# Linear attention feeding a gated MLP on one core: attention on head pairs with nine tokens per partition, the next batch placed by hand between the MLP's groups

## The chip, the cores and the metric

The kernel runs on one core of one Trainium2 chip. The metric is the device time of one execution in microseconds, given as the median of several runs. Profiles come from one profiled execution. Engines are called as the profile calls them: PE (TensorE matmuls), PEld (its weight loads), DVE (VectorE), ACT (ScalarE), POOL (GpSimd) and SP (SyncE, which here only issues DMAs).

## What is computed

Eight batches of eight heads, 576 tokens and 64 features go through an attention without softmax, in which relu of q and of k is weighted by the cosine and the sine of the token's position; the result, with its heads side by side, is the input x (4608 x 512) of a two-layer MLP ("MoE" in the names) with a swish between.

```python
theta = np.pi / 2.0 * np.arange(S) / S                      # S = 576
def phi(x, c, s):
    r = np.maximum(x, 0.0)
    return np.concatenate([r * c, r * s], axis=-1)          # 64 -> 128 features
q_p, k_p = phi(q, cos_w, sin_w), phi(k, cos_w, sin_w)
kv = np.einsum('bhsf,bhsd->bhfd', k_p, v)
z = np.sum(k_p, axis=2)
num = np.einsum('bhsf,bhfd->bhsd', q_p, kv)
den = np.einsum('bhsf,bhf->bhs', q_p, z)[..., None] + 1e-06
x = (num / den).transpose(0, 2, 1, 3).reshape(B * S, H * D)  # 4608 x 512
h = x @ w_in                                                # w_in 512 x 2048
out = (h * (1.0 / (1.0 + np.exp(-beta * h)))) @ w_out       # w_out 2048 x 512
```

Inputs and the output are float32; the matmuls of both kernels run in bfloat16. Both compute `Silu(beta * h)` and divide row j of `w_out` by `beta[j]` when it is cast.

## The kernel before

**Attention** (`attention_batch`, L111). One batch is taken in five pieces of up to 128 tokens (the last has 64), with a token on each partition and the eight heads side by side. Per piece, k, v and q are loaded in runs of 64 floats (L127; k on SP's queue, v on ACT's, q on both in turn). ACT writes `k_p` with two relu activations, one scaled by cosine, one by sine (L137, L139); DVE does the same for `q_p` (L143, L146) and casts v (L151), and POOL sets a 65th column to one, which yields z. For each head PE adds `k_p`ᵀ `v` to `kv_ps` (L156, 65 columns) and transposes `q_p` (L166), and DVE copies the transposes out (L174). Behind the five pieces `kv_ps` is copied to SBUF (L179); then each piece and head has a matmul `num_ps` (L189, 65 columns), a reciprocal of its 65th column (L198), the division (L204), four transposes of `x_sb` (L220) and ACT's copy into `xt_all` (L228), the whole transposed x.

**MoE** (`moe_chunk`, L233). A chunk is 512 tokens, and there are nine. For each of 16 slices of 128 hidden features, four matmuls of 512 columns fill `h_ps` (L239, two PSUM buffers) and ACT's Silu makes `g_t` (L247). Then each of the chunk's four groups of 128 tokens has 16 matmuls into `o_ps` (L257, one PSUM buffer, but in the last two chunks two that belonged to `num_ps`), a copy by DVE (L265) and an output DMA on POOL's queue (L266).

**Weights.** `load_w_in` (L94) and `load_w_out` (L103) load float32 pieces into two staging buffers and DVE casts them (L100, L108); `w_out` comes on POOL's queue in 16 pieces.

**Order.** The calls at the end (L268 to L281) are: w_in, batch 0, w_out, batch 1, and then each batch followed by those chunks whose tokens are ready. That order is only a priority: the framework's scheduler arranges the instructions of each engine and moves matmuls of later work up into gaps.

Of the kernel before, what the change touches and what calls it, by code (L numbers as in the profile page):

```python
# [13 lines left out]
ALU = mybir.AluOpType  # L14

USE_XBAR_X = False
# [3 lines left out]
def kernel(  # L20
# [9 lines left out]
):  # L30
    nc = tc.nc

    B, H, S, D = q.shape
    P = 128
    NT = B * S
# [4 lines left out]
    HG = H // 2  # L40
    NCH = (S + P - 1) // P
    SC = [min(P, S - n * P) for n in range(NCH)]
    TCH = 512
    NTC = NT // TCH
    TT = TCH // P

    const_pool = ctx.enter_context(tc.tile_pool(name="const", bufs=1))
    xt_pool = ctx.enter_context(tc.tile_pool(name="xt", bufs=1))
    win_pool = ctx.enter_context(tc.tile_pool(name="win", bufs=1))
    wout_pool = ctx.enter_context(tc.tile_pool(name="wout", bufs=1))  # L50
    kvz_pool = ctx.enter_context(tc.tile_pool(name="kvz", bufs=2))

    raw_pool = ctx.enter_context(tc.tile_pool(name="raw", bufs=4))
    kp_pool = ctx.enter_context(tc.tile_pool(name="kp", bufs=3))
    qpt_pool = ctx.enter_context(tc.tile_pool(name="qpt", bufs=2))
    xsb_pool = ctx.enter_context(tc.tile_pool(name="xsb", bufs=3))
    rden_pool = ctx.enter_context(tc.tile_pool(name="rden", bufs=4))
    gt_pool = ctx.enter_context(tc.tile_pool(name="gt", bufs=18))
    osb_pool = ctx.enter_context(tc.tile_pool(name="osb", bufs=3))

    kv_psum_pool = ctx.enter_context(tc.tile_pool(name="kvps", bufs=1, space=bass.MemoryType.PSUM))
    tps_psum_pool = ctx.enter_context(tc.tile_pool(name="tps", bufs=1, space=bass.MemoryType.PSUM))
    num_psum_pool = ctx.enter_context(tc.tile_pool(name="numps", bufs=1, space=bass.MemoryType.PSUM))
    moeh_psum_pool = ctx.enter_context(tc.tile_pool(name="moehps", bufs=2, space=bass.MemoryType.PSUM))
    moeo_psum_pool = ctx.enter_context(tc.tile_pool(name="moeops", bufs=1, space=bass.MemoryType.PSUM))

    ident = const_pool.tile([P, P], BF16)
    make_identity(nc, ident)

    iota_t = const_pool.tile([P, NCH], FP32)  # L70
    nc.gpsimd.iota(iota_t, pattern=[[P, NCH]], base=0, channel_multiplier=1,
                   allow_small_or_imprecise_dtypes=True)

    ANG = math.pi / (2.0 * S)
    sin_cols = const_pool.tile([P, NCH], FP32)
    cos_cols = const_pool.tile([P, NCH], FP32)
    halfpi = const_pool.tile([P, 1], FP32)
    nc.vector.memset(halfpi, math.pi / 2.0)
    zero_b = const_pool.tile([P, 1], FP32)
    nc.vector.memset(zero_b, 0.0)  # L80
    nc.scalar.activation(sin_cols, iota_t, AF.Sin, bias=zero_b, scale=ANG)
    nc.scalar.activation(cos_cols, iota_t, AF.Sin, bias=halfpi, scale=-ANG)

    beta_sb = const_pool.tile([P, JT], FP32)
    nc.sync.dma_start(out=beta_sb, in_=moe_beta.rearrange("(j p) -> p j", p=P))
    rbeta_sb = const_pool.tile([P, JT], FP32)
    nc.vector.reciprocal(rbeta_sb, beta_sb)

    xt_all = xt_pool.tile([P, MI, NT], BF16, name="xt_all")

    win_bf = []
    wout_bf = []

    def load_w_in(staging):  # L94
        for mi in range(MI):
            w_stage = staging.tile([P, DF], FP32, name="w_stage", tag="w_stage")
            eng = nc.sync if mi % 2 == 0 else nc.scalar
            eng.dma_start(out=w_stage, in_=moe_w_in[mi * P : (mi + 1) * P, :])
            wt = win_pool.tile([P, DF], BF16, name=f"win{mi}")
            nc.vector.tensor_copy(wt, w_stage)  # L100
            win_bf.append(wt)

    def load_w_out(staging):  # L103
        for jc in range(JT):
            wo_stage = staging.tile([P, DM], FP32, name="wo_stage", tag="wo_stage")
            nc.gpsimd.dma_start(out=wo_stage, in_=moe_w_out[jc * P : (jc + 1) * P, :])
            wo = wout_pool.tile([P, DM], BF16, name=f"wout{jc}")
            nc.vector.tensor_scalar_mul(wo, wo_stage, rbeta_sb[:, jc : jc + 1])  # L108
            wout_bf.append(wo)

    def attention_batch(b):  # L111
        kv_ps = [
            kv_psum_pool.tile([P, HG, D + 1], FP32, name=f"kv_ps{g}", tag=f"kv_ps{g}")
            for g in range(2)
        ]
        qpt_sb = qpt_pool.tile([P, H, S], BF16, name="qpt_sb")

        for n in range(NCH):
            sc = SC[n]
            raws = {}  # L120
            for name, src, eng in (
                ("k", k, nc.sync),
                ("v", v, nc.scalar),
                ("q", q, nc.sync if n % 2 == 0 else nc.scalar),
            ):
                t = raw_pool.tile([P, H, D], FP32, name=f"raw_{name}", tag=f"raw_{name}")
                eng.dma_start(  # L127
                    out=t[:sc],
                    in_=src[b, :, n * P : n * P + sc, :].rearrange("h p d -> p h d"),
                )  # L130
                raws[name] = t
            raw_k = raws["k"][:sc]
            raw_q = raws["q"][:sc]
            raw_v = raws["v"][:sc]

            k_p = kp_pool.tile([P, H, 2, D], BF16, name="k_p", tag="k_p")
            nc.scalar.activation(k_p[:sc, :, 0, :], raw_k, AF.Relu,  # L137
                                 scale=cos_cols[:sc, n : n + 1])
            nc.scalar.activation(k_p[:sc, :, 1, :], raw_k, AF.Relu,  # L139
                                 scale=sin_cols[:sc, n : n + 1])  # L140

            q_p = kp_pool.tile([P, H, 2, D], BF16, name="q_p", tag="q_p")
            nc.vector.tensor_scalar(q_p[:sc, :, 0, :], raw_q,  # L143
                                    scalar1=cos_cols[:sc, n : n + 1], scalar2=0.0,
                                    op0=ALU.mult, op1=ALU.max)
            nc.vector.tensor_scalar(q_p[:sc, :, 1, :], raw_q,  # L146
                                    scalar1=sin_cols[:sc, n : n + 1], scalar2=0.0,
                                    op0=ALU.mult, op1=ALU.max)

            v_sb = kp_pool.tile([P, H, D + 1], BF16, name="v_sb", tag="v_sb")  # L150
            nc.vector.tensor_copy(v_sb[:sc, :, 0:D], raw_v)  # L151
            nc.gpsimd.memset(v_sb[:sc, :, D : D + 1], 1.0)

            for h in range(H):
                g, hg = divmod(h, HG)
                nc.tensor.matmul(  # L156
                    kv_ps[g][:, hg, :],
                    lhsT=k_p[:sc, h, :, :],
                    rhs=v_sb[:sc, h, :],
# [152 lines left out]
```

## Time and profile before

| | us |
|---|---|
| median of 3 runs | 384.47 |
| lowest, highest run | 381.54, 386.7 |
| profiled execution, span from first to last instruction | 381.9 |
| PE busy in it (2272 matmuls) | 322.9 |
| DVE busy (395 instructions) | 150.5 |
| ACT busy (268 instructions) | 169.3 |
| POOL busy (99 instructions) | 36.6 |

The span is the profiled execution's own time; it lies among the times of the runs, and no time around it is given apart from it. PE's busy row counts a matmul until its modelled end, so that matmuls overlap in it and a full row still can hide short waits. For those the starts of successive matmuls are compared. 46.53 MB go through the DMA queues, 115472 of 119340 packets being smaller than 512 bytes.

### The profile page before, as it was taken

How to read it: one execution, taken by the hardware profiler on the slowest of the kernel's cores; microseconds unless marked ns; L12 is line 12 of the kernel's file. 1: busy time of each engine (PE TensorE's matmuls, PEld its weight loads, DVE VectorE, ACT ScalarE, POOL GpSimd, SP SyncE). 2: the span in 40 equal slices, each digit the busy share in tenths (PEclk: the TensorE clock that was granted, in tenths of full speed). 3: DMA queues.
4: the chain of work that ended last, by engine and by line, in shares of the span. 5: the costliest groups of instructions: out<-in, count | busy, mean ns of one | idle time of the engine just before them, and what ended most of it. 6: DMA issues, size and time to landing. Idle time of an engine off the chain costs nothing.

```text
span 381.9 us, 5842 instructions
## 1 busy us (share of the span) xinstructions
PE 322.9 (85%) x2272; PEld 165.8 (43%) x2272; DVE 150.5 (39%) x395; ACT 169.3 (44%) x268; POOL 36.6 (10%) x99
## 2 busy tenths in 40 slices
PE   0130265799989999999999999999999999999993
PEld 0020243555445555455545545554555444444441
DVE  0551484753664268255405743750346011020020
ACT  1133046077447734770753595257306613604600
POOL 2021131000110020001001100110010011011011
PEclk9999999599999999999999999999999999999999
DMA  8999969533996399469208956410010011011011
GB/s 259 313 278 223 235 178 225 80 70 87 234 245 127 70 223 231 96 155 232 60 0 192 197 101 135 124 57 0 29 55 30 0 56 56 0 57 55 1 57 55
DMA packets 119340, 46.53 MB, mean 122 GB/s; under 512 B 115472, under 2 KB 115472, under 8 KB 118800
## 3 DMA queue, kind: packets, MB, share of 16 engines
q1 hardware_dynamic: 60720, 16.79, 23.0%
q10 hardware_dynamic: 54432, 15.73, 20.2%
q0 software_dynamic: 4160, 13.63, 11.0%
q8 instruction: 18, 0.29, 0.3%
q14 instruction: 10, 0.08, 0.1%
HBM read 36.71 MB, written 9.44 MB: 121 GB/s over the span
## 4 chain that ended last, share of the span: by engine, by line
PE 48%; issue 28%; DMA 14%; DVE 5%; POOL 2%; ACT 1%; POOLq 0%; ACTq 0%; DVEq 0%
PE h_ps L239 22%; PE o_ps L257 17%; DMA wo_stage<-in_moe_w_out_dram 10%; DMA raw_q<-in_q_dram 4%; PE num_ps L189 3%; PE t_ps L166 3%; PE t_ps L220 2%; POOL out_dram L266 2%; PE kv_ps L156 2%; DVE o_sb L265 1%; DVE q_p L143 1%; DVE q_p L146 1%; DVE qpt_sb L174 1%; DVE wout L108 1%; DVE x_sb L204 0%
## 5 line engine op out<-in xcount | busy, mean ns | idle before, releaser
L239 PE MATMUL h_ps<-xt_all,win 128*128 128x512 bf16 x576 | 148.2, 384 | 0.4 <-ACT g_t L247 0.3
L247 ACT ACTIVATE g_t<-h_ps,beta_sb 128x512 bf16<-128x512 f32 x144 | 98.5, 688 | 97.6 <-PE h_ps L239 93.4
L257 PE MATMUL o_ps<-wout,g_t 128*128 128x512 bf16 x448 | 105.8, 379 | 0.3
L257 PEld LDWEIGHTS <-g_t 128*128 128x128 bf16 x576 | 56.0, 98 | 65.8 <-issue 0.9
L239 PEld LDWEIGHTS <-win 128*128 128x128 bf16 x576 | 52.2, 98 | 56.4 <-issue 9.5
L265 DVE COPY o_sb<-o_ps 128x512 f32<-128x512 f32 x28 | 19.3, 689 | 81.3 <-PE o_ps L257 81.3
L166 PE MATMUL t_ps<-ident,q_p 128*128 128x128 bf16 (+1 forms) x320 | 27.6, 231 | 27.9 <-DVE q_p L143 17.5
L137 ACT ACTIVATE k_p<-raw_k,cos_cols 128x512 bf16<-128x512 f32 (+1 forms) x40 | 28.7, 717 | 46.4 <-PE kv_ps L156 22.2
L228 ACT COPY xt_all<-t_ps 128x512 bf16<-128x512 bf16 (+1 forms) x40 | 21.7, 542 | 44.0 <-PE t_ps L220 34.9
L174 DVE COPY qpt_sb<-t_ps 128x1024 bf16<-128x1024 bf16 (+1 forms) x40 | 25.2, 630 | 35.8 <-PE t_ps L166 35.6
L166 PEld LDWEIGHTS <-q_p 128*128 128x128 bf16 (+1 forms) x320 | 21.2, 106 | 35.6 <-DVE q_p L143 17.5
L156 PE MATMUL kv_ps<-v_sb,k_p 128*128 128x65 bf16 (+1 forms) x320 | 20.0, 206 | 19.4 <-DVE v_sb L151 17.9
L266 POOL DMA_DIRECT2D out_dram<-o_sb x36 | 19.7, 547 | 156.0 <-DVE o_sb L265 123.3
L204 DVE TENSOR_TENSOR x_sb<-num_ps,rden 128x256 bf16<-128x256 f32 (+1 forms) x80 | 31.2, 414 | 1.0
L139 ACT ACTIVATE k_p<-raw_k,sin_cols 128x512 bf16<-128x512 f32 (+1 forms) x40 | 28.4, 711 | 0.0
L257 PE MATMUL o_ps_tail<-wout,g_t 128*128 128x512 bf16 x128 | 28.0, 379 | 0.0
L156 PEld LDWEIGHTS <-k_p 128*128 128x128 bf16 (+1 forms) x320 | 16.3, 105 | 26.7 <-issue 17.6
L189 PE MATMUL num_ps<-kvz_sb,qpt_sb 128*128 128x65 bf16 (+1 forms) x320 | 24.0, 203 | 1.2 <-DVE x_sb L204 0.8
L265 DVE COPY o_sb<-o_ps_tail 128x512 f32<-128x512 f32 x8 | 5.5, 691 | 49.2 <-PE o_ps_tail L257 49.2
L189 PEld LDWEIGHTS <-qpt_sb 128*128 128x128 bf16 (+1 forms) x320 | 17.9, 106 | 8.6 <-DVE x_sb L204 3.1
L220 PE MATMUL t_ps<-ident,x_sb 128*128 128x128 bf16 (+1 forms) x160 | 19.0, 223 | 3.1 <-DVE x_sb L204 3.0
L143 DVE TENSOR_SCALAR q_p<-raw_q,cos_cols 128x512 bf16<-128x512 f32 (+1 forms) x40 | 18.9, 475 | 6.6 <-DMA raw_q<-in_q_dram 6.6
(23 smaller groups left out, 99.5 us busy)
## 6 DMA issues: line engine op xcount, KB each, us to landing
out_dram<-o_sb POOLq DMA_DIRECT2D x36, 256.0 KB, 3.0
raw_v<-in_v_dram ACTq DMA_DIRECT2D x32, 256.0 KB, 4.7
raw_k<-in_k_dram SPq DMA_DIRECT2D x32, 256.0 KB, 6.8
wo_stage<-in_moe_w_out_dram POOLq DMA_DIRECT2D x16, 256.0 KB, 5.9
raw_q<-in_q_dram ACTq DMA_DIRECT2D x16, 256.0 KB, 5.0
raw_q<-in_q_dram SPq DMA_DIRECT2D x16, 256.0 KB, 6.8
w_stage<-in_moe_w_in_dram SPq DMA_DIRECT2D x2, 1024.0 KB, 8.3
w_stage<-in_moe_w_in_dram ACTq DMA_DIRECT2D x2, 1024.0 KB, 8.1
```

What stands on the lines that cost most here:

```text
L137: nc.scalar.activation(k_p[:sc, :, 0, :], raw_k, AF.Relu, scale=cos_cols[:sc, n : n + 1])
L139: nc.scalar.activation(k_p[:sc, :, 1, :], raw_k, AF.Relu, scale=sin_cols[:sc, n : n + 1])
L156: nc.tensor.matmul(kv_ps[g][:, hg, :], lhsT=k_p[:sc, h, :, :], rhs=v_sb[:sc, h, :], start=(n == 0 and hg == 0), stop=(n == NCH - 1 and hg ...
L166: nc.tensor.matmul(qpt_ps[:, h, 0:sc], lhsT=q_p[:sc, h, :, :], rhs=ident[:sc, :sc], is_transpose=True, start=(h == 0), stop=(h == H - 1),)
L174: nc.vector.tensor_copy(qpt_sb[:, :, n * P : n * P + sc], qpt_ps[:, :, 0:sc])
L189: nc.tensor.matmul(num_ps[g][:sc, hg, :], lhsT=qpt_sb[:, h, n * P : n * P + sc], rhs=kvz_sb[:, h, :], start=(hg == 0), stop=(hg == HG - 1),)
L204: nc.vector.tensor_tensor(x_sb[:sc, hs, :], num_ps[g][:sc, :, 0:D], rb, op=ALU.mult,)
L239: nc.tensor.matmul(h_ps, lhsT=win_bf[mi][:, jt * P : (jt + 1) * P], rhs=xt_all[:, mi, t0 : t0 + TCH], start=(mi == 0), stop=(mi == MI - 1),)
L247: nc.scalar.activation(g_t, h_ps, AF.Silu, scale=beta_sb[:, jt : jt + 1])
L257: nc.tensor.matmul(o_ps, lhsT=g_tiles[jt][:, tt * P : (tt + 1) * P], rhs=wout_bf[jt], start=(jt == 0), stop=(jt == JT - 1),)
L265: nc.vector.tensor_copy(o_sb, o_ps)
L266: nc.gpsimd.dma_start(out=out[t0 + tt * P : t0 + (tt + 1) * P, :], in_=o_sb)
```

## The change

Everything in the kernel function is rewritten; the computation stays.

- **Layout.** Heads are taken in pairs: head 2j on partitions 0 to 63, head 2j + 1 on 64 to 127. Each partition holds nine consecutive tokens of its head, so that one piece of a load is 9 x 64 floats, 2304 bytes. Tokens are worked on in the order n, p (token 9p + n), and the output's view undoes that: a group of 128 goes out in two DMAs of 64 rows. All loads are issued on SP's queue, the outputs on POOL's, and from chunk 6 on SP's.
- **Weights of position.** Cosine and sine are put on v rather than on k (`v_scale`, nine instructions each, with the cosine or sine itself as 65th column), so k and q need one relu each. On the q side the cosine falls out of the quotient: `rt_c` is the transposed relu of q, and `rt_s` the same times a tangent, which is multiplied in while the transpose leaves PSUM. `den` gets an epsilon divided by the cosine.
- **Matmuls per batch.** 18 transposes of q (a pair of heads in each), 36 kv matmuls with 64 rows and 260 columns (both heads times cosine and sine; a mask then zeroes the products of unlike heads), 40 `num` matmuls of 130 columns, and 20 transposes of x as before.
- **Buffers.** `xt` is a tile per chunk (three buffers). Attention shares one PSUM pool of two double banks, `h_ps` and `o_ps` have two banks each. The o copies are ACT's, the x copies DVE's (in batch 0 ACT's).
- **Order.** `manual_schedule`: each engine executes in the order written. Batch 0 comes first; w_in is cast beside it. Chunk 0 has 32 slots (16 h groups, 16 quarters of o groups), between which stand the casts of w_out and the parts of batch 1 (`early`); a rest of batch 1 follows it. In chunks 1 to 6 the parts of batch c + 1 stand at the slots given in `att_units`; chunks 7 and 8 have none.

The diff, cut to its core. Removed are the functions printed above; added are:

```diff
+    raw_pool = ctx.enter_context(tc.tile_pool(name="raw", bufs=2))
+    stage = ctx.enter_context(tc.tile_pool(name="stage", bufs=4))
+    xt_pool = ctx.enter_context(tc.tile_pool(name="xt", bufs=3))
+    hps_pool = ctx.enter_context(tc.tile_pool(name="hps", bufs=2, space=PSUM))
+    ops_pool = ctx.enter_context(tc.tile_pool(name="ops", bufs=2, space=PSUM))
+    att_pool = ctx.enter_context(tc.tile_pool(name="att", bufs=2, space=PSUM))
+    ctx.enter_context(tc.manual_schedule())
...
+    def raw_view(src, b):
+        return src[b].rearrange("(j g) (p n) d -> (g p) j (n d)", g=2, n=NQ)
...
+    for jp in range(2):
+        load_half("q", q, jp)
+    for jp in range(2):
+        load_half("v", v, jp)
+        load_half("k", k, jp)
...
+    def q_relu(b, jp=None, eng=None):
...
+            nc.vector.tensor_scalar(o, i, scalar1=0.0, scalar2=None, op0=ALU.max)
...
+    def v_scale(b, cs, jp=None, eng=None):
...
+        for n in range(NQ):
+            nc.vector.tensor_scalar(vb[:, n, cs, :, 0:D], rv[:, :, n, :],
+                                    scalar1=t[:, n : n + 1], scalar2=None, op0=ALU.mult)
...
+    def q_transpose(b, u, eng="dve"):
+        n0, n1 = (0, 4) if u == 0 else (4, 8) if u == 1 else (8, 9)
+        nn = n1 - n0
+        if u != 1:
+            qts[b] = att_pool.tile([P, 2, 1024], BF16, name="qt_ps", tag="att")
...
+        for jp in range(2):
+            src = t[:, jp].rearrange("q n (g p) -> q n g p", g=2)
...
+            if eng == "act":
+                nc.scalar.copy(dst_c, src)
+            else:
+                nc.vector.tensor_copy(dst_c, src)
+            nc.vector.tensor_tensor(dst_s, src, tan_v, op=ALU.mult)
...
+    def kv_mm(b, jp):
+        t = att_pool.tile([P, 2, 512], FP32, name="kv_ps", tag="att")
+        kvs[b, jp] = t
+        for n in range(NQ):
+            for g in range(2):
+                hs = slice(g * half, (g + 1) * half)
+                nc.tensor.matmul(
+                    t[:, g, 0 : 4 * E],
+                    lhsT=rk[hs, n, 2 * jp : 2 * jp + 2, :],
+                    rhs=vb[hs, n, :, 2 * jp : 2 * jp + 2, :],
+                    start=(n == 0), stop=(n == NQ - 1))
...
+    def num(b, ci):
+        m = MCI[ci]
+        t = att_pool.tile([P, 2, 512], FP32, name="num_ps", tag="att")
+        for g in range(2):
+            for jp in range(2):
+                for cs, rt in ((0, rt_c), (1, rt_s)):
+                    nc.tensor.matmul(
+                        t[:m, g, jp * 2 * E : (jp + 1) * 2 * E],
+                        lhsT=rt[:, g, jp, 2 * ci : 2 * ci + m // half, :],
+                        rhs=kv[:, g, jp, cs, :],
+                        start=(cs == 0), stop=(cs == 1))
...
+        nc.vector.tensor_scalar(den[:m], nv[:, :, :, D], scalar1=epsc[:m, ci : ci + 1],
+                                scalar2=None, op0=ALU.add)
+        nc.vector.reciprocal(rden[:m], den[:m])
...
+    def att_units(b):
+        u = [
+            (0, lambda: q_relu(b)),
+            (1, lambda: v_scale(b, 0)),
+            (3, lambda: q_transpose(b, 0)),
+            (4, lambda: k_relu(b)),
+            (5, lambda: q_transpose(b, 1)),
+            (6, lambda: v_scale(b, 1)),
+            (7, lambda: q_transpose(b, 2)),
+            (12, lambda: kv_build(b, 0)),
+            (14, lambda: kv_build(b, 1)),
+        ]
+        at = 16
+        for ci in range(NCI):
+            u.append((at + 2 * ci, lambda ci=ci: num(b, ci)))
+        for ci in range(NCI):
+            u.append((at + 2 * ci + 3, lambda ci=ci: x_transpose(b, ci)))
...
+    warm_pe(12)
+    q_relu(0, 0, "act")
+    q_relu(0, 1, "act")
+    q_transpose(0, 0, "act")
+    q_transpose(0, 1, "act")
+    warm_pe(4)
+    v_scale(0, 0, 0)
+    v_scale(0, 1, 0, nc.gpsimd)
+    k_relu(0, 0, "act")
+    q_transpose(0, 2, "act")
+    kv_mm(0, 0)
+    v_scale(0, 0, 1)
+    v_scale(0, 1, 1, nc.gpsimd)
+    k_relu(0, 1, "act")
+    kv_mask(0, 0)
+    kv_mm(0, 1)
+    kv_mask(0, 1)
+    num(0, 0)
+    num(0, 1)
+    x_transpose(0, 0, "act")
+    cast_w("in", 0, "act")
+    num(0, 2)
+    x_transpose(0, 1, "act")
+    num(0, 3)
+    x_transpose(0, 2, "act")
+    x_transpose(0, 3, "act")
+    cast_w("in", 1)
+    load_w("out", 0)
+    load_w("out", 1)
+    load_batch(1, "k")
+    cast_w("in", 2)
+    load_batch(1, "v")
+    load_w("out", 2)
+    cast_w("in", 3)
+    load_batch(1, "q")
+    load_w("out", 3)
+    early = {
+        3: lambda: num(0, 4),
+        5: lambda: x_transpose(0, 4),
+        7: lambda: cast_w("out", 0),
+        10: lambda: cast_w("out", 1),
+        12: lambda: k_relu(1),
+        15: lambda: v_scale(1, 0),
+        18: lambda: v_scale(1, 1),
+        20: lambda: cast_w("out", 2),
+        21: lambda: kv_build(1, 0),
+        23: lambda: kv_build(1, 1),
+        24: lambda: q_relu(1),
+        25: lambda: cast_w("out", 3),
+        26: lambda: q_transpose(1, 0),
+        27: lambda: q_transpose(1, 1),
+        28: lambda: num(1, 0),
+        29: lambda: num(1, 1),
+        30: lambda: x_transpose(1, 0),
+    }
...
+    q_transpose(1, 2)
+    num(1, 2)
+    x_transpose(1, 1)
+    num(1, 3)
+    x_transpose(1, 2)
+    num(1, 4)
+    x_transpose(1, 3)
+    x_transpose(1, 4)
+    load_batch(2)
+    for c in range(1, NTC):
+        if c + 2 < B:
+            load_batch(c + 2)
+        units = att_units(c + 1) if c + 1 < B else []
+        for slot in range(32):
+            if slot < 16:
+                h_group(c, slot)
             else:
+                o_part(c, (slot - 16) // 4, slot % 4)
+            while units and units[0][0] <= slot:
+                units.pop(0)[1]()
```

466 lines of the change are left out of this document (251 added, 215 removed).

## Prediction

> **What bounds the kernel now.** I read the page's slices first, then a table by stage, then the timeline of TensorE.
>
> ```profile
> span 381.9 us, 5842 instructions
> ...
> PE   0130265799989999999999999999999999999993
> ...
> PEclk9999999599999999999999999999999999999999
> ...
> GB/s 259 313 278 223 235 178 225 80 70 87 234 245 127 70 223 231 96 155 232 60 0 192 197 101 135 124 57 0 29 55 30 0 56 56 0 57 55 1 57 55
> ```
>
> A slice is 9.55 us. TensorE is full from the ninth slice on and mostly idle before it, so there are two regimes. The stage table cuts at the first MoE matmul (57), at the point where PE stays full (86) and at its end (376):
>
> ```profile
> core 0: us, PE busy (x) PEld busy (x) DVE busy (x) ACT busy (x) POOL busy (x), PEclk, DMA share, GB/s
> 0.00:57.00 57.00, 13.21 (x139) 10.11 (x140) 25.46 (x64) 13.86 (x22) 11.17 (x29) 1.00 1.04 247
> 57.00:86.00 29.00, 22.63 (x188) 13.11 (x189) 17.06 (x47) 14.23 (x23) 1.81 (x7) 0.82 0.71 127
> 86.00:271.00 185.00, 183.35 (x1375) 94.84 (x1374) 85.64 (x235) 103.52 (x166) 14.72 (x45) 1.00 0.63 132
> 271.00:376.00 105.00, 103.75 (x575) 47.77 (x572) 22.38 (x49) 37.70 (x57) 8.36 (x17) 1.00 0.10 38
> ...
> 57.00:86.00 29.00, 14.42 (x40) 3.61 (x40) 0.82 0.71 127
> ...
> 57.00:86.00 29.00, 1.61 (x6) 0.60 (x7) 0.82 0.71 127
> ```
>
> The last two rows are the same table for the h matmuls (L239) and the o matmuls (L257) alone: by 86 us only 46 of the 1152 MoE matmuls have run. In the first 57 us the DMA engines are full (share 1.04) at 247 GB/s. What one matmul costs in a full queue comes from the timeline, start to start, since the printed duration of one overlaps the next:
>
> ```profile
> 271.31 0.42 PE L156 MATMUL kv_ps<-v_sb,k_p 128*128 128x65 bf16 x8
> 271.57 0.61 PE L166 MATMUL t_ps<-ident,q_p 128*128 128x128 bf16 x8
> 272.01 0.19 PE L156 MATMUL kv_ps<-v_sb,k_p 128*128 128x65 bf16 x1
> 272.25 3.61 PE L257 MATMUL o_ps<-wout,g_t 128*128 128x512 bf16 x16
> ...
> 276.65 3.61 PE L257 MATMUL o_ps<-wout,g_t 128*128 128x512 bf16 x16
> ...
> 285.20 0.43 PE L156 MATMUL kv_ps<-v_sb,k_p 64*128 64x65 bf16 x8
> 285.56 0.82 PE L239 MATMUL h_ps<-xt_all,win 128*128 128x512 bf16 x3
> ...
> 332.43 13.98 PE L257 MATMUL o_ps_tail<-wout,g_t 128*128 128x512 bf16 x64
> 346.24 9.33 PE L239 MATMUL h_ps<-xt_all,win 128*128 128x512 bf16 x40
> ```
>
> A 512-column matmul takes 13.81/64 = 0.2158 us, a 65-column one 0.26/8 = 0.033 (0.045 on 64 rows), a 128-column transpose 0.44/8 = 0.055. So 1106 matmuls from 86 on are 238.7 us, and six batches of attention (40 + 40 + 40 + 20 small ones, (40 + 20) x 0.055 + 80 x 0.033 = 5.9) are 36: 274 of the 290 us from 86 to 376. The other 16 are waits that PE's busy row doesn't show, such as the o groups, which start 4.40 apart for 3.45 of work (272.25 to 276.65): they have one PSUM buffer. The kernel loses some 70 us before 86, then is bound by TensorE.
>
> **The change, term by term.** The new order is written out: TensorE starts chunk 0 after batch 0 alone, and then carries 1152 x 0.2158 = 248.6 us of MoE, seven batches of attention, its waits, and the end.
>
> Rows for the work on the other engines:
>
> ```profile
> L265 DVE COPY o_sb<-o_ps 128x512 f32<-128x512 f32 x28 | 19.3, 689 | 81.3 <-PE o_ps L257 81.3
> L204 DVE TENSOR_TENSOR x_sb<-num_ps,rden 128x256 bf16<-128x256 f32 x64 | 24.8, 414 | 0.6
> L143 DVE TENSOR_SCALAR q_p<-raw_q,cos_cols 128x512 bf16<-128x512 f32 x32 | 15.2, 476 | 6.6 <-DMA raw_q<-in_q_dram 6.6
> L100 DVE CAST win<-w_stage 128x2048 bf16<-128x2048 f32 x4 | 4.9, 1247 | 6.5 <-DMA w_stage<-in_moe_w_in_dram 6.3
> L174 DVE COPY qpt_sb<-t_ps 128x512 bf16<-128x512 bf16 x8 | 3.3, 417 | 0.1
> L198 DVE RECIPROCAL rden<-num_ps 128x4 f32<-128x4 f32 x64 | 10.3, 173 | 4.7 <-PE num_ps L189 4.1
> L137 ACT ACTIVATE k_p<-raw_k,cos_cols 128x512 bf16<-128x512 f32 x32 | 22.9, 717 | 37.8 <-PE kv_ps L156 18.8 <-DMA raw_k<-in_k_dram 9.3 <-DVE v_sb L151 7.8
> L228 ACT COPY xt_all<-t_ps 128x512 bf16<-128x512 bf16 x32 | 18.7, 585 | 43.0 <-PE t_ps L220 34.0 <-DVE x_sb L204 8.3 <-PE num_ps L189 0.7
> L228 ACT COPY xt_all<-t_ps 128x256 bf16<-128x256 bf16 x8 | 2.9, 369 | 1.0 <-PE t_ps L220 1.0
> L247 ACT ACTIVATE g_t<-h_ps,beta_sb 128x512 bf16<-128x512 f32 x144 | 98.5, 688 | 97.6 <-PE h_ps L239 93.4 <-PE o_ps L257 4.0
> masks.py:199 POOL TENSOR_SCALAR_AFFINE_SELECT ident<-ident 128x128 bf16<-128x128 bf16 x1 | 0.3, 283 | 0.0
> L81 ACT ACT_TABLE_LOAD x1 | 1.3, 1283 | 4.9 <-issue 4.9
> ```
>
> VectorE, one source from SBUF: 476 ns for 512, 1247 for 2048, so 0.22 us + 0.50 ns per element. ScalarE: (585 - 369)/256 = 0.84 ns per element. A relu of a whole batch (2304 elements) is then 1.38 us on VectorE; one `v_scale` instruction (256) 0.35. The multiply by `tanr` (512, PSUM, two tensors) isn't in the trace: between 0.54 (414 + 256 x 0.50) and 0.83 (twice 414); I take 0.69, the PSUM copy of that size.
>
> 1. **Start of chunk 0.** Batch 0 is q, v and k, 3.54 MB, in 2304-byte pieces. ScalarE first loads two tables (2.6 us), does the sines and copies the tangents out: free at about 8.2, when q (1.18 MB) has landed. Then: two half relus, 717 + 640 x 0.84 = 1.26 each, 10.7; transposes, 11.5; their eight evacuations on ScalarE (0.59) and VectorE (0.69) side by side, 14.2; v times cosine (1152 elements, 1.35), 15.6; 18 kv matmuls on a cool clock, mask, 19.3; the second pair, 21.9; `num` (each 2 x 0.17 + 0.69 = 1.03 on VectorE) and x transposes with the 2.0 us cast of w_in 0 among their copies, 28.3. **T0 = 28.5 us**, bounds 24 (half the relus and evacuations overlapped) and 36 (clock lowered, as in the second stage of the table, where it averages 0.82 amid gaps, and every second evacuation waited for). GpSimd's two multiplies (1152) cost between 1.35 (VectorE's) and 2.5 (0.283/128 per element) and lie beside this. The w_in loads are hidden: 7.7 MB at 247 GB/s land by 33, the last cast at 34.6, and slot 12, which wants it, comes at 28.5 + 12 x 0.863 = 38.9. Without that cover each us late counts in full.
>
> 2. **Attention per batch on TensorE.** 18 transposes instead of 40: 0.99. 20 x transposes: 1.1. 40 `num` matmuls of 130 columns: between 0.045 and 0.0625 (two of the 65-column ones and a quarter of a 512) each; 0.056 is 2.24. The 36 kv matmuls of 64 rows and 260 columns: 260/512 x 0.2158 = 0.110 each, so 4.0 one after the other, 2.0 if the upper and lower half of the rows ran at once; no row has a matmul on the upper half. Nothing in the rows leans to an end, so 3.0. Sum 7.3, against 5.9 before: dearer on TensorE by 1.4. Times seven is **51.3**, with 0.7 for what is left of batch 0.
>
> On the kv term the Trainium skill ("TensorE: Matmul & The Clock Gate", Part 3, row/col tiling) says that matmuls on different row strips run concurrently, which would make it 2.0 and the sum 7 us less. Against it, the Trainium skill ("TensorEngine Tiling (Array Packing)", Key Properties) says that a change of tiling mode drains the array; by this trace's tail of a lone matmul (0.38 long, 0.216 apart) four changes a batch would give 4.7 us back. No run here shows either yet.
>
> 3. **Waits in chunk 0.** All of w_out and batch 1 (15.5 MB from the start) must be in by slot 28. At 313 GB/s (second slice) that is 51.5 us with 2 for the first landing; slot 28 comes at 28.5 + 24.2 + 6 = 59, so it is hidden; at 247 it would be 8 us late. After slot 31 eight units stand with no MoE between them: VectorE has 1.0 + 3 x 1.03 + 4 to 5 x 0.42 = 6.2 us there, with PE waiting at each step. With about 2 us where `num(1, 0)` waits for the evacuations just queued: **7**, bounds 3 and 15.
>
> 4. **Waits in chunks 1 to 6.** VectorE runs ahead of TensorE with q relu and the first `v_scale`. Transposes of slot 3 end 4.0 us into the chunk; then on VectorE 2.0 for their evacuation (two of 417, two of 0.69, slightly overlapped), 1.4 for k, 2.0 for the second transposes, 2.6 for the second `v_scale`: 12.0. `kv_build` stands at 13 x 0.863 + 1.0 = 12.2. It just fits; **0.5 a chunk, 3 in all**, bounds 0 and 24 (4 a chunk if VectorE's strided forms took twice the slope; the waiting instruction holds everything behind it in PE's queue). ScalarE takes the o copies: 16 x 0.688 + 4 x 0.69 = 13.8 of 35 us, hidden, and o has two PSUM buffers, so the 0.95 us per o group goes.
>
> 5. **End.** Before:
>
> ```profile
> 375.30 0.69 DVE L265 COPY o_sb<-o_ps_tail 128x512 f32<-128x512 f32 x1 [2.76 <-PE o_ps_tail L257]
> 376.28 0.54 POOL L266 DMA_DIRECT2D out_dram<-o_sb  x1 [2.92 <-DVE o_sb L265]
> ...
> out_dram<-o_sb POOLq DMA_DIRECT2D x36, 256.0 KB, 3.0
> ```
>
> The last copy starts at 375.3 and the span ends 6.6 later; the copy is halved, and SP issues two DMAs: **6**, bounds 4 and 7.
>
> Sum: 28.5 + 248.6 + 51.3 + 0.7 + 7 + 3 + 6 = 345.1 us, against the span of 381.9. The median of the runs shown is 384.47, 2.6 above that span; so the forecast is **347.7 us**.
>
> **Rivals.**
>
> *Overlapped halves and no waits* (0.25). kv at 2.0 (7 less), the steady waits gone (3 less), 2 less behind chunk 0: 335.7. For it: the two halves write different PSUM banks, and the estimates in step 4 meet. Against it: no row shows it.
>
> *VectorE late* (0.12). Step 4's upper bound: 24 instead of 3 gives 368.7. For it: the new outputs are strided, and kv's place has 0.2 us to spare. Against it: `q_p` (L143) is strided as well, and is in the 0.50 ns line.
>
> *Loads keep the gain* (0.05), so that the change doesn't do what it says. If 2304-byte pieces came no faster than the 178 GB/s of the sixth slice, 15.5 MB would be in at 89; 89 + 2 cast + 3.5 for four slots + 7 behind them puts chunk 1 at 101.5, where steps 1 to 3 put it at 71.1 (28.5 + 27.6 + 7.3 + 0.7 + 7): 378. For it: DMA share 1.04 now. Against it: 313 in a slice already, with half of its pieces at 256 bytes.
>
> *In-order waits at every unit* (0.03), the slow side. In the automatic order other work goes in front of a late one; in a written order nothing does. The trace has the price of such a wait:
>
> ```profile
> PE t_ps L220 <- DVE x_sb L204: 3.0, 4, 1.1
> ```
>
> If 12 of a batch's units waited 1.1 us each, 13.2 a chunk, six chunks would cost 76 more: 424. It decides from 6.6 us a chunk on (36.8 + 3 spread over six). Against it: two slots, 1.7 us of matmuls, lie between most units and the VectorE work they want.
>
> **How the numbers follow.** The forecast has 0.55, with a range of its own of 338 to 358 (kv 2 to 4, T0 and chunk 0 within a few us). The others have 0.25, 0.12, 0.05 and 0.03. About 2%, under 377 or over 392, is what a measurement of this kernel can tell: faster is 0.55 + 0.25 + 0.12 = 0.92; the load case lies at the bound and counts as the same, 0.05; slower 0.03. The range takes in the overlap case from below and most of VectorE late: 328 to 370.
>
> **What would show it.** Right: the first h matmul at 24 to 36 us; PE full in every slice from then on, but for one dip of 3 to 15 us behind chunk 0 at 60 to 75; chunks 1 to 6 at 34 to 37 us each, the last two at 27.6; o groups without the 0.95 us. kv's price is read start to start: 0.11 a matmul or half of that. Wrong: a wait over 2 us at the kv matmuls for `vb` in every chunk; T0 past 40; w_out landing past 60; or a granted clock under 1 in the steady part.

## The result, and the profile after

The changed kernel takes 357.13 us (median of four runs, 356.56 to 358.02) against 384.19 for the kernel before in the same comparison: a ratio of 0.930 (95% interval 0.926 to 0.935). The forecast was 347.7, in a range of 328 to 370. The page of the profiled execution, in the same 40 slices (now 8.9 us each):

```profile
span 356.3 us, 5161 instructions
...
PE   4665999869999999999999999999999999999994
...
PEclk9865899978999999999999999999999999999999
...
GB/s 268 393 210 122 362 390 383 307 222 138 262 29 54 175 262 29 50 177 262 29 50 178 262 32 46 45 0 31 44 46 0 32 59 29 2 59 61 2 57 61
```

TensorE is full from the fifth slice on, where it was from the ninth, with one dip in the ninth. In the row PEclk, the clock granted to TensorE is at half in the fourth slice and below full in the ones beside it. How far the MoE had come by 86 us is read from a table by stage, for the h matmuls (L348) and then the o matmuls (L363) alone; the second pair of numbers counts weight loads, one a matmul:

```profile
core 0: us, PE busy (x) PEld busy (x), PEclk, DMA share, GB/s
...
34.40:86.00 51.60, 23.73 (x85) 9.29 (x87) 0.90 0.85 311
...
34.40:86.00 51.60, 14.69 (x62) 5.89 (x64) 0.90 0.85 311
```

That is 87 + 64 = 151 matmuls of 512 columns where the kernel before had 46. The 105 more, at the 0.222 us that one takes on average in the last two chunks (28.38/128, below), are 23 of the 25.6 us by which the spans differ. The rest of the run is **not** faster. The timeline of TensorE:

```profile
34.41 0.59 PE L348 MATMUL h_ps<-xt,win 128*128 128x512 bf16 x1 [0.67 <-ACT xt L336]
...
78.00 0.61 PE L348 MATMUL h_ps<-xt,win 128*128 128x512 bf16 x1
...
93.43 1.18 PE L276 MATMUL kv_ps<-vb,rk 64*128 64x260 bf16 x18
94.55 1.90 PE L348 MATMUL h_ps<-xt,win 128*128 128x512 bf16 x8
...
99.23 0.22 PE L302 MATMUL num_ps<-kv,rt_c 128*128 128x130 bf16 x1
...
99.70 1.89 PE L363 MATMUL o_ps<-wout,g_t 128*128 128x512 bf16 x8
...
115.96 3.69 PE L348 MATMUL h_ps<-xt,win 128*128 128x512 bf16 x16
...
151.64 3.69 PE L348 MATMUL h_ps<-xt,win 128*128 128x512 bf16 x15
...
294.36 14.73 PE L348 MATMUL h_ps<-xt,win 128*128 128x512 bf16 x62
308.92 13.98 PE L363 MATMUL o_ps<-wout,g_t 128*128 128x512 bf16 x63
322.74 14.73 PE L348 MATMUL h_ps<-xt,win 128*128 128x512 bf16 x63
```

Chunk 1 begins at 78.00, chunk 2 at 115.96, chunk 3 at 151.64, and chunk 7, the first without attention, at 294.36. So chunk 2 takes 35.68 us with a whole batch of attention in it, and chunk 7 takes 28.38. Six such chunks and 338 further matmuls at 0.222 would take 289 us; the kernel before needed 290 for the same work, the 1106 matmuls and six batches from 86 to 376.

### The profile page after: what moved, and what is told of

It reads as the page before. It is cut to its first block, busy times and chain, and to the rows that moved or that the text cites. A ratio compares the mean times of both kernels' runs of the same rounds, so it can differ in the third digit from the quotient of the medians.

```text
span 356.3 us, 5161 instructions
## 1 busy us (share of the span) xinstructions
PE 328.2 (92%) x2048; PEld 166.1 (47%) x2085; DVE 168.6 (47%) x443; ACT 135.3 (38%) x204; POOL 34.3 (10%) x66
## 3 DMA queue, kind: packets, MB, share of 16 engines
q0 software_dynamic: 2304, 6.29, 6.8%
## 4 chain that ended last, share of the span: by engine, by line
PE 86%; DVE 9%; ACT 2%; issue 1%; ACTq 0%; DVEq 0%
PE h_ps L348 34%; PE o_ps L363 34%; PE num_ps L302 6%; PE kv_ps L276 5%; DVE rt_s L266 3%; PE qt_ps L253 3%; PE xt_ps L327 2%; DVE rt_c L265 2%; PE warm_ps L412 1%; DVE x_sb L315 1%; ACT rt_c L263 1%; DVE vb L231 1%; PE tan_ps L183 1%; DVE wout L120 0%; DVE kv L284 0%
## 5 line engine op out<-in xcount | busy, mean ns | idle before, releaser
L348 PE MATMUL h_ps<-xt,win 128*128 128x512 bf16 x556 | 137.6, 387 | 2.1 <-ACT xt L336 0.7
L363 PE MATMUL o_ps<-wout,g_t 128*128 128x512 bf16 x559 | 134.6, 379 | 1.0 <-issue 0.2
L351 ACT ACTIVATE g_t<-h_ps,beta 128x512 bf16<-128x512 f32 x144 | 99.0, 687 | 66.5 <-PE h_ps L348 66.5
L348 PEld LDWEIGHTS <-win 128*128 128x128 bf16 x576 | 55.2, 99 | 71.0 <-issue 17.1
L363 PEld LDWEIGHTS <-g_t 128*128 128x128 bf16 x576 | 53.0, 98 | 53.5 <-issue 0.4
L373 ACT COPY o_sb<-o_ps 128x512 f32<-128x512 f32 x35 | 20.5, 587 | 128.1 <-PE o_ps L363 124.2
L266 DVE TENSOR_TENSOR rt_s<-qt_ps,tanr 128x512 bf16<-128x512 bf16 (+1 forms) x48 | 26.2, 546 | 8.6 <-ACT rt_c L263 8.6
L315 DVE TENSOR_TENSOR x_sb<-num_ps,rden 128x512 bf16<-128x512 f32 (+1 forms) x40 | 27.6, 689 | 1.4
L302 PE MATMUL num_ps<-kv,rt_c 128*128 128x130 bf16 (+1 forms) x160 | 24.6, 230 | 3.7 <-DVE x_sb L315 2.6
L284 DVE TENSOR_TENSOR kv<-kv_ps,mask 128x520 bf16<-128x520 f32 x16 | 11.2, 699 | 34.4 <-PE kv_ps L276 34.4
L302 PE MATMUL num_ps<-kv,rt_s 128*128 128x130 bf16 (+1 forms) x160 | 24.7, 231 | 0.0
L276 PE MATMUL kv_ps<-vb,rk 64*128 64x260 bf16 x288 | 19.8, 279 | 3.1 <-DVE vb L231 3.1
L338 DVE COPY xt<-xt_ps 128x512 bf16<-128x512 bf16 (+1 forms) x40 | 14.2, 363 | 10.3 <-PE xt_ps L327 10.0
L302 PEld LDWEIGHTS <-rt_s 128*128 128x128 bf16 (+1 forms) x160 | 16.7, 104 | 4.4 <-issue 1.5
```

Source lines behind the costliest of these rows:

```text
L266: nc.vector.tensor_tensor(dst_s, src, tan_v, op=ALU.mult)
L276: nc.tensor.matmul(t[:, g, 0 : 4 * E], lhsT=rk[hs, n, 2 * jp : 2 * jp + 2, :], rhs=vb[hs, n, :, 2 * jp : 2 * jp + 2, :], start=(n == 0), s ...
L302: nc.tensor.matmul(t[:m, g, jp * 2 * E : (jp + 1) * 2 * E], lhsT=rt[:, g, jp, 2 * ci : 2 * ci + m // half, :], rhs=kv[:, g, jp, cs, :], st ...
L315: nc.vector.tensor_tensor(x_sb[:m].rearrange("q j g e -> q g j e"), nv[:, :, :, 0:D], rden[:m].unsqueeze(3).to_broadcast([m, 2, 4, D]), op ...
L348: nc.tensor.matmul(h_ps, lhsT=win[jt // 4][:, mi, (jt % 4) * P : (jt % 4 + 1) * P], rhs=xt[:, mi, :], start=(mi == 0), stop=(mi == MI - 1))
L351: nc.scalar.activation(g_t, h_ps, AF.Silu, scale=beta[:, jt : jt + 1])
```

## The experiments

All ratios are against the kernel before, measured beside it; the changed kernel's is 0.930 (0.926 to 0.935). Differences from the changed kernel are taken from the ratios: two ratios 0.010 apart differ by 3.8 us.

**The order of the start: batch 1 ahead of chunk 0.**

```diff
+    for slot in sorted(early):
+        early[slot]()
+    q_transpose(1, 2)
+    num(1, 2)
...
     for slot in range(32):
         if slot < 16:
             h_group(0, slot)
         else:
             o_part(0, slot % 4, (slot - 16) // 4)
-        if slot in early:
-            early[slot]()
-    q_transpose(1, 2)
-    num(1, 2)
...
```

> Batch 1 is finished before chunk 0 begins, as the kernel before has it; all else stays. Theory (the whole gain is that the MoE starts after one batch and fills the time in which batch 1 and w_out arrive): the first h matmul moves from 34 to 65 or 70 us, chunk 0 takes 28 us behind it, and chunk 1 starts at 93 to 98 instead of 78: 372 to 378, that is most of the gain over the kernel before is gone. Rival (the gain comes from cheaper attention in the steady part): the start costs less than 8 us, under 365.

379.5 us, ratio 0.986 (0.981 to 0.990), 1.5 us above the theory's range. Four fifths of the gain are gone (0.056 of 0.070 in the ratio), with everything else of the change in place. In TensorE's timeline of this kernel chunk 0 begins at 70.48 and chunk 1 at 100.81:

```profile
70.48 16.69 PE L348 MATMUL h_ps<-xt,win 128*128 128x512 bf16 x64
...
100.81 3.69 PE L348 MATMUL h_ps<-xt,win 128*128 128x512 bf16 x16
```

That is 22.8 us later than 78.00; the time rose by 21. Most of the gain is the start, as the theory says; the rival (cheaper attention) is out. No run puts this order into the kernel before, so how much of the rewriting the early start needs is open.

**The interleaving: all of a batch behind slot 31.**

```diff
         for slot in range(32):
...
-            while units and units[0][0] <= slot:
-                units.pop(0)[1]()
+        while units:
+            units.pop(0)[1]()
```

> In chunks 1 to 6 all parts of the next batch stand behind slot 31 instead of between the slots; the rest of the order stays. Theory (the interleaving hides a chain of VectorE work of about 20 us a batch, of which TensorE needs only 6.7): 11 to 14 us a chunk come to light, and the clock falls behind them: 357 + 6 x 13 + some us, 430 to 450. Rival (VectorE runs ahead during the chunk, so that only the chain of num and x transposes is left): 5 to 6 us a chunk, about 390.

456.6 us, ratio 1.186 (1.181 to 1.192): 98 us more, 16.4 a chunk, above the theory's range and far from the rival's. A table by stage cut at one batch of attention (108.0 to 130.5) and at the first half of the chunks before and behind it:

```profile
core 0: us, PE busy (x) PEld busy (x) DVE busy (x) ACT busy (x) POOL busy (x), PEclk, DMA share, GB/s
78.00:95.00 17.00, 17.00 (x67) 6.91 (x66) 3.79 (x11) 10.57 (x16) 0.00 (x0) 0.87 0.21 70
...
108.00:130.50 22.50, 13.72 (x117) 9.06 (x114) 16.22 (x43) 0.58 (x1) 1.03 (x2) 0.61 0.39 121
130.50:147.00 16.50, 16.50 (x69) 6.77 (x68) 3.92 (x11) 10.51 (x16) 0.00 (x0) 0.91 0.22 72
```

VectorE works 16.2 of the 22.5 us. From its first transposes, at 108.3, to the next h group, at 130.5, the batch takes 22.2 us, where its matmuls alone need 6.7 (worked out below): 15.5 of the 16.4. The rest goes with the clock, which is 0.61 there and 0.91 in the h phase behind it, and which the forecast of this run had put at only a few us in all.

**Lower and upper rows in turn.**

```diff
-        for n in range(NQ):
-            for g in range(2):
+        for g in range(2):
+            for n in range(NQ):
```

> The 18 kv matmuls of a pair of heads run first on the lower 64 rows (nine), then on the upper 64 (nine), instead of in turn. In the changed kernel they are 0.062 us apart. Theory: lower and upper half overlap, and that is why they are nearer to half of 0.110 than to 0.110; with nine of a half in a row nothing can overlap, so they should be 0.11 apart, 0.86 us more per 18, 12 us in 14 of them (batch 0 runs on a low clock): about 369 us against 357.1. Rival: 64 rows are cheap by themselves (a term that has nothing to do with halves); then the spacing stays at 0.06 and the time at 357.

365.3 us, ratio 0.948 (0.944 to 0.952): 6.8 us more where 12 were expected. The 18 matmuls in this kernel's timeline:

```profile
93.21 1.75 PE L276 MATMUL kv_ps<-vb,rk 64*128 64x260 bf16 x18
94.90 1.90 PE L348 MATMUL h_ps<-xt,win 128*128 128x512 bf16 x8
```

94.90 - 93.21 = 1.69 us, against 94.55 - 93.43 = 1.12 in the changed kernel. The halves do overlap: in the changed kernel two matmuls of 282 ns each stand within 0.29 us. The rival had 1.12 here too. The size was missed since nine and nine still overlap in part: by the single starts in the trace, the first matmul of the upper half starts at 93.79, beside the sixth of the lower half, and the sum is 14 steps of 0.11 and not 18.

**The automatic order.** One line, `ctx.enter_context(tc.manual_schedule())`, is removed.

> The same instructions, but the framework's scheduler chooses the order of each engine, as in the kernel before. Theory (the gain is the earlier start of the MoE, which the smaller loads and the head pairs allow, and the written order adds no more than the automatic one does in the steady part): 357 within 8, with the first h matmul at 30 to 38 us. Rival: the written order carries the gain; then it falls back to 375 to 385, with the h matmuls late or with attention stalls between chunks.

362.7 us, ratio 0.941 (0.936 to 0.946), the first h matmul at 37.5. Fixing the order is worth 1.2% here, not the gain. For the rival (375 to 385) nothing is left. The scheduler still takes the written order as its priority, so this run shows that the order needn't be fixed, not that it doesn't matter.

**Loads in 256-byte pieces.**

```diff
-        raws[name, 0] = raw_pool.tile([P, 4, NQ, D], FP32, ...)
+        raws[name, 0] = raw_pool.tile([P, 4, NQ, D + 4], FP32, ...)[:, :, :, 0:D]
...
-        nc.sync.dma_start(out=raws[name, 0][:, js].rearrange("q j n d -> q j (n d)"), in_=raw_view(src, 0)[:, js, :])
+        for j in (2 * jp, 2 * jp + 1):
+            nc.sync.dma_start(out=raws[name, 0][:, j], in_=raw_view(src, 0)[:, j])
```

> q, k and v are loaded in pieces of 256 bytes, as in the kernel before, instead of 2304: the rows of the destination are 68 floats apart, and each load is four DMAs of one pair of heads. Nothing else changes. Theory (the smaller number of pieces is one of the two things that let chunk 0 start early): the first 60 us move bytes at 220 to 270 GB/s instead of 340, batch 0 lands some 4 us later and batch 1 some 5 us later, chunk 1 starts 5 to 8 us later: 362 to 366. Rival (the start is bound by the chain of engines behind the loads, which has its data in time either way): within 2 us of 357.

360.5 us, ratio 0.936 (0.931 to 0.941): 2.2 us more, between the two, with an interval that touches the changed kernel's. Chunk 0 begins at 32.54, before the 34.41 of the changed kernel, while chunk 1 begins at 80.81 instead of 78.00:

```profile
32.54 3.69 PE L344 MATMUL h_ps<-xt,win 128*128 128x512 bf16 x16 [0.67 <-ACT xt L332]
...
80.81 5.66 PE L344 MATMUL h_ps<-xt,win 128*128 128x512 bf16 x16
```

So the stretch from the one to the other grew from 43.6 to 48.3 us. In it VectorE waits for v of batch 1 and then for the last piece of w_out, which it didn't in the changed kernel:

```profile
48.92 2.46 DVE L234 TENSOR_SCALAR vb<-raw_v,cos 128x256 bf16<-128x256 f32 x9 [4.15 <-DMA raw_v<-in_v_dram]
...
63.21 1.67 DVE L116 TENSOR_SCALAR wout<-w_stage,rbeta 128x512 bf16<-128x512 f32 x4 [3.72 <-DMA w_stage<-in_moe_w_out_dram]
```

The start can't be compared as cleanly. Batch 0 came more slowly, at 223 GB/s from 11 to 15 us where the changed kernel had 398, but from 24 to 34 us the clock was 1.00, where the changed kernel had 0.50:

```profile
11.00:15.00 4.00, 1.26 (x18) 1.02 (x17) 1.38 (x2) 1.18 (x3) 2.11 (x1) 1.00 1.32 223
...
24.00:28.00 4.00, 1.94 (x27) 1.52 (x28) 2.85 (x7) 1.00 (x2) 0.00 (x0) 1.00 1.05 389
```

So the time has two effects of opposite sign in it: some 5 us lost in chunk 0 to late loads, as the theory has it, and a start on a higher clock. That the start hangs on the chain of engines, as the rival has it, fits the trace, but this run doesn't show it apart from the clock.

**A tile of its own for the second transposes.**

```diff
-        if u != 1:
-            qts[b] = att_pool.tile([P, 2, 1024], BF16, name="qt_ps", tag="att")
-        bank = 1 if u == 1 else 0
+        qts[b] = att_pool.tile([P, 2, 1024], BF16, name="qt_ps", tag="att")
+        bank = 0
```

> The second group of q transposes (u = 1) gets a PSUM tile of its own, where it shared one with the first group, in another bank. Theory: TensorE's waits at the second group (2.7 us in batch 0, 1.5 in batch 1, 0.31 in each later one) come from the shared tile, whose readers must be done before it is written again, although the banks differ; they go: about 2 to 4 us less, 353 to 355. Rival: the wait is for something else on VectorE (its evacuations in order), and comes back at the next transposes: 357, or more, since a third tile of the pool of two is now wanted.

350.0 us, ratio 0.908 (0.903 to 0.913): 8.6 us less, twice what the theory gave. The waits of the changed kernel that it was aimed at (sum in us, count, longest):

```profile
PE qt_ps L253 <- DVE rt_s L266: 6.1, 8, 2.7
```

Of these 1.4 us are left (one wait, at the third transposes of batch 0, where the rival had it). Most of the rest of what was saved goes with the clock, though no run separates the two. In the changed kernel the clock is 0.50 in the stages from 24.0 to 34.4, from 34.4 to 38 and from 78 to 82:

```profile
24.00:34.40 10.40, 6.47 (x52) 4.94 (x49) 6.42 (x15) 4.04 (x5) 0.00 (x0) 0.50 0.26 99
34.40:38.00 3.60, 3.37 (x8) 1.32 (x9) 2.07 (x2) 0.69 (x1) 0.00 (x0) 0.50 0.68 238
...
74.00:78.00 4.00, 2.22 (x27) 1.53 (x24) 2.93 (x9) 0.00 (x0) 0.00 (x0) 0.74 0.59 231
78.00:82.00 4.00, 3.78 (x11) 1.49 (x11) 3.91 (x12) 1.06 (x2) 0.00 (x0) 0.50 0.26 56
```

In this kernel it is 0.95 from 24 to 28 us and 0.50 from 28 to 34, and the last of these stages has the whole clock:

```profile
74.00:78.00 4.00, 4.00 (x26) 2.00 (x24) 3.85 (x12) 2.75 (x4) 0.00 (x0) 1.00 0.53 159
78.00:82.00 4.00, 3.95 (x27) 2.14 (x26) 4.00 (x8) 2.75 (x4) 0.00 (x0) 1.00 0.45 150
```

By spans (346.5 against 356.3) chunk 0 begins 4.0 us earlier, chunk 1 5.0, and chunk 1 itself takes 35.5 instead of 38.0.

**No matmuls on zeros.** Both `warm_pe` calls are removed.

> The 16 matmuls on zeros at the start, whose result nothing reads, are left out. Theory: they only delay the first transposes (the half relus are done at 9.75 us, the zeros' matmuls end at 11.8), and the granted clock has fallen to 0.50 by 24 us anyway: 1 to 2 us less, about 355.5. Rival: they keep the clock up for the transposes and the first kv matmuls; then these take twice as long and the time is 357 to 359.

355.6 us, ratio 0.924 (0.919 to 0.929): 2.5 us less, but the interval overlaps the changed kernel's, so that the time alone can't tell them apart. The trace has the first transposes at 8.76 instead of 11.63, and chunk 0 at 30.70 instead of 34.41:

```profile
8.76 0.61 PE L253 MATMUL qt_ps<-ident,qb 128*128 128x128 bf16 x4 [1.64 <-ACT qb L213]
...
30.70 0.59 PE L348 MATMUL h_ps<-xt,win 128*128 128x512 bf16 x1 [0.67 <-ACT xt L336]
```

The clock between 24 and 28 us was 0.99, not 0.50; from 28 to 34 it was 0.50 in both. So the matmuls on zeros delay the transposes, and without them the clock is no lower. Whether their absence is also why it stayed up until 28 is open, since with them it was 0.95 there in the run before this one.

**Batch 1 between the slots of chunk 0.**

```diff
-    load_w("out", 0)
-    load_w("out", 1)
-    load_batch(1, "k")
...
+    load_batch(1)
+    for i in range(4):
+        load_w("out", i)
...
+    early = att_units(1) + [
+        (3, lambda: num(0, 4)),
+        (5, lambda: x_transpose(0, 4)),
+        (9, lambda: cast_w("out", 0)),
+        (15, lambda: cast_w("out", 1)),
+        (19, lambda: cast_w("out", 2)),
+        (23, lambda: cast_w("out", 3)),
+    ]
```

> Batch 1 is loaded before w_out, and its parts stand between the slots of chunk 0 as those of later batches do, with nothing behind slot 31; the four casts of w_out stand at slots 9, 15, 19 and 23. Theory (the 8.7 us of waits in chunk 0 and the low clock behind them come from batch 1 being late, since its loads wait for the staging buffers of w_in): chunk 1 starts at about 71 instead of 78 and runs on the full clock: 346 to 349. Rival (VectorE has too much to do in chunk 0, or w_out comes late, so that the waits only move): 354 to 358.

350.6 us, ratio 0.911 (0.906 to 0.916), 7.5 us less; 1.6 above the theory's range. Chunk 0 takes 39.4 instead of 43.6 us, and chunk 1 is back at 35.7. The loads and the places of the parts were changed together, so their shares are open:

```profile
33.30 5.41 PE L348 MATMUL h_ps<-xt,win 128*128 128x512 bf16 x16 [0.67 <-ACT xt L336]
...
72.70 3.69 PE L348 MATMUL h_ps<-xt,win 128*128 128x512 bf16 x16
```

**The three together.** The last three edits in one kernel.

> The tile of its own for the second transposes, no matmuls on zeros, and batch 1 between the slots of chunk 0, in one kernel. Alone they gave 7 to 8, 2 and 6 to 7 us, but the first and the third both take the wait and the low clock behind chunk 0, and the first and the second both shorten batch 0. Theory: the first h matmul at 28 to 30 us, chunk 1 at 65 to 67, chunks 1 to 6 at 35.3 each, then 56.7 and 6: 338 to 344. Rival (they take the same waits and don't add up): 348 to 350, no better than the best of them alone.

344.6 us, ratio 0.897 (0.893 to 0.900): just above the theory's range, 3.6% under the changed kernel. Chunk 0 begins at 30.16 and chunk 1 at 69.64, where the theory had 65 to 67. They don't add up (18.6 us singly, 13 together), as the theory had it; the rival (no better than the best of them) is out.

**The start of batch 0 as well.**

```diff
+        for first in range(2):
+            for u in (first, 1 - first):
...
+                    if u == first:
+                        nc.scalar.copy(rt_c[:, :, jp, n0:n1, :].rearrange("q g n p -> q n g p"), src)
+                    else:
+                        nc.vector.tensor_tensor(
...
+        if b == 0 and ci < 4:
+            tv = ops_pool.tile([P, 1024], BF16, name="xt_ps", tag="o_ps")[:, 0 : MI * P]
```

> As the run before, and in batch 0 ScalarE copies one group of transposes while VectorE multiplies the other, then they change over, and the x transposes take PSUM from the o pool, which is idle then. Theory (in the changed kernel the two engines took the same tile in turn, which is why the evacuations lasted to 18.7 us where the prediction had 14.2, and num had to wait for the copies of the x transposes before it got a tile): 2.5 to 4 us less than the run before it. Rival (v and its multiplications set the pace there, not the transposes): within 1 us of it.

344.6 us, ratio 0.896 (0.894 to 0.899): no gain. But chunk 0 begins at 26.13 instead of 30.16, as the theory has it; the 4 us are lost again within the chunk, at the second transposes of batch 1:

```profile
26.13 3.69 PE L373 MATMUL h_ps<-xt,win 128*128 128x512 bf16 x15 [0.68 <-ACT xt L361]
...
37.59 1.04 PE L252 MATMUL qt_ps<-ident,qb 128*128 128x128 bf16 x8 [4.88 <-DVE rt_s L265]
...
69.70 3.69 PE L373 MATMUL h_ps<-xt,win 128*128 128x512 bf16 x15
```

The chain of waits goes back from there to VectorE's scaling of v, and from it to the load of v, which lands at 33.2:

```profile
17.16 16.04 DMA raw_v<-in_v_dram
33.20 0.03 issue
33.22 2.46 DVE vb L238 x9
35.68 0.33 DVE rt_c L264
```

**v of batch 1 later in VectorE's queue.**

```diff
-    early = att_units(1) + [
+    early = [({1: 8, 6: 9}.get(s, s), f) for s, f in att_units(1)] + [
...
-        (9, lambda: cast_w("out", 0)),
+        (14, lambda: cast_w("out", 0)),
```

> As the run before (which brought the first h matmul to 26.1 us but no gain), with the two scalings of v of batch 1 at slots 8 and 9 of chunk 0 instead of 1 and 6, and the first cast of w_out at 14 instead of 9. Theory (VectorE's queue stood at the scaling of v until v of batch 1 landed at 33.2, and the evacuations of the transposes stood behind it, which cost TensorE 4.9 and 2.6 us and the clock): these waits go, chunk 1 starts at 63 to 66 instead of 69.7: 338 to 341. Rival (the bytes themselves are late, whatever the order): the wait moves to the kv matmuls or to w_out, and the time stays within 1.5 us of 344.6.

342.4 us, ratio 0.889 (0.885 to 0.892), the fastest here, though short of the theory's 338 to 341: the 4.9 us wait is gone, but chunk 1 begins at 67.9 and not at 63 to 66. Part of that is the clock: from 28 to 30 us it was 0.50, where the run before had 1.00, and 14 of the first h matmuls took 4.5 us. The rival (within 1.5 us of the run before) is out.

**Four buffers for h.** In chunks 7 and 8 every second h group takes its PSUM from attention's pool.

```diff
+        if c >= B - 1 and jt % 2:
+            h_ps = att_pool.tile([P, 2, TCH], FP32, name="h_ps", tag="att")[:, 0]
+        else:
+            h_ps = hps_pool.tile([P, TCH], FP32, name="h_ps", tag="h_ps")
```

> In chunks 7 and 8, where attention is over, every second h group takes its PSUM from the pool of attention, so that h has four buffers in turn instead of two. All else stays. In the changed kernel 64 h matmuls take 14.56 us there, 0.2275 apart, where 64 o matmuls take 13.82, 0.216 apart; every second group of four starts 0.135 late. Theory (each h group waits for ScalarE to release one of two buffers): the lateness goes, 64 h matmuls take 13.8, and the two chunks save 1.5 us: the last h matmul to the end is unchanged, 355.6 us. Rival (the lateness is TensorE's own, at a change of PSUM bank or at the weights of w_in): still 14.5, and 357.

356.2 us, ratio 0.928 (0.922 to 0.934), which can't be told from the changed kernel by time. The trace settles it:

```profile
293.65 13.98 PE L351 MATMUL h_ps<-xt,win 128*128 128x512 bf16 x62
307.47 13.98 PE L366 MATMUL o_ps<-wout,g_t 128*128 128x512 bf16 x63
321.28 13.98 PE L351 MATMUL h_ps<-xt,win 128*128 128x512 bf16 x63
```

64 h matmuls take 307.47 - 293.65 = 13.82 us, 0.216 each, as the theory has it; with two buffers they took 14.56. (The counts are of records; a few are missing.)

## Why the prediction was right, and where its terms were off

The mechanism was right: the MoE starts after one batch, TensorE is full from then on but for one dip, and the steady part takes as long as before. The first run above shows that the start carries most of the gain. The number was less good than the mechanism: 357.1 lies 9.4 us above the forecast, at the very edge of its own range of 338 to 358. The terms, by spans:

| | forecast | measured |
|---|---|---|
| start of chunk 0 | 28.5 | 34.4 |
| chunk 0 with batch 1 and what follows it | 42.6 | 43.6 |
| chunks 1 to 6 | 212.4 | 216.4 |
| chunks 7 and 8 | 55.2 | 56.7 |
| end | 6 | 5.2 |

- **Step 1 was short by 5.9 us.** It let ScalarE and VectorE evacuate the transposes of batch 0 side by side, 14.2. In the trace they take turns on the tile. The chain of the changed kernel, from the first copy on:

```profile
12.28 0.59 ACT rt_c L263
12.89 0.70 DVE rt_s L266
13.62 0.59 ACT rt_c L263
14.21 0.02 issue
14.24 0.70 DVE rt_s L266
14.94 0.04 issue
14.98 1.03 PE qt_ps L253 x8
```

  The second group of transposes waits for all four, and the last multiplication ends at 18.7, 4.5 us late. The other part is `num` and the x transposes, 9.3 us from the second mask to the first h matmul instead of 6.4: half of the clock, and PSUM tiles that wait for the copies of the x transposes. (Between the two, 1.3 us were won.) On top of the three edits, giving each engine a group of its own and the x transposes other PSUM brought the start from 30.2 to 26.1, under the forecast.
- **The rate of the MoE was mis-sized.** 0.2158 us came from o groups and was used for h as well. With two PSUM buffers h takes 14.56/64 = 0.2275, 0.75 us a chunk and 6.7 in nine. The trace before had it: of the rows quoted there, the last begins an h phase (346.24), and it wasn't followed to its end, where the next o matmul starts at 361.28; that is 0.235 each, a wait of 0.27 included. The run with four buffers shows the cause.
- **Attention per batch, 7.3, was too dear.** kv is 36 x 0.062 = 2.2 instead of 3.0 (1.12 us for 18); `num` is 0.47/8 = 0.059 each (99.23 to 99.70), 2.3 where 2.24 was taken. In all 6.7. The 3.0 was a middle between two prices that no row told apart. The rule of the Trainium skill ("TensorE: Matmul & The Clock Gate", Part 3) that row strips run concurrently agrees with this trace, in which a pair of matmuls takes 0.11. The drain that the Trainium skill ("TensorEngine Tiling (Array Packing)", Key Properties) sets against it did not show as a loss that eats the gain: 18 matmuls with the step back to full rows take 1.12, and nine pairs at 0.11 are 0.99. The rival of overlapped halves had nearly the right price, 2.0 for 2.2; the waits that it dropped stayed.
- **The waits of chunk 0 were right** in size: of its 43.6 us, 28.4 are MoE, 7.4 attention and some 2 the low clock on the first h groups, which leaves 6 for the 7 forecast. The waits of TensorE over 0.3 us that the trace lists there add up to 4.4. In step 3, the 8 us late at 247 GB/s should be 6 (15.5 MB and 2 us make 64.8, against 59); the sum doesn't use it.
- **The steady waits were right**: 35.68 less 28.4 and 6.7 is 0.6 a chunk, for 0.5; half of it is the 0.31 of the shared tile. VectorE met its place at `kv_build`: no wait for `vb` in chunks 1 to 6. The 2.6 of step 4 for the second `v_scale` doesn't follow from its own price (nine times 0.35 is 3.15), but nine take 2.46 in the chain quoted above.
- **The clock was left out.** But for batch 0's first kv matmuls, it was given to the start's upper bound alone; it also costs some 2 us in chunk 0 and 2.3 in chunk 1 (37.96 against 35.68). So one sign of being wrong did come, a granted clock under 1 in the steady part (0.50 from 78 to 82 us), and chunk 1 lies outside the 34 to 37 us that would show it right.

Errors of both signs met, and that the forecast came as near as it did is in part luck: rate, start and clock made some 17 us more, attention 4 less, the waits of chunk 0 and the end 2 less; by spans 356.3 against 345.1. Another 1.8 is how a span was made a time: 2.6 was added, but each run of the changed kernel is only 1.7 us longer than its span (358.02 against 356.3). Of the rivals, the late VectorE and the waits at every unit did not come, nor did loads at 178 GB/s: from 6 to 21 us they ran at 371 to 398.

## What to carry to other kernels

When a profile shows an engine that is full for most of the span, look at how long it takes to become full, and ask what is the least that it needs to begin; here that was worth 23 of 25.6 us, and moving it back cost 21. An order that hides a chain of another engine is worth the length of that chain and the clock with it, even where the hidden engine is far from busy. Take a rate from each kind of loop apart: two phases with the same instruction can differ by 5% through their buffers.

## What the runs showed of the hardware

- Two matmuls on 64 rows and 260 columns each, on different halves of the rows and into different PSUM banks, cost about as much as one: a pair starts every 0.11 us, as far apart as two of the same half. That is 0.062 us each in turn, the step back to full rows included, against 0.094 with nine of each half in a row.
- The clock falls without a long pause. From 72 to 76 us TensorE was busy for 1.86 of 4.0 us, and its longest wait was 1.06 us. From 74 to 78 the granted clock was 0.74, and from 78 to 82, with TensorE busy for 3.78 of 4.0 us, 0.50. The Trainium skill ("TensorE: Matmul & The Clock Gate", Why this matters for your kernels) warns of pauses over about 3 us; here shorter ones at half load were enough.
- Loads in pieces of 2048 and 2304 bytes ran at 371 to 398 GB/s (the changed kernel, 6 to 21 us). Batch 0 in pieces of 256 bytes ran at 223 to 229 (6 to 18 us of the kernel with small pieces), with the DMA engines no less busy.
